# Third tiles of at most 64 tokens at 320 columns with stacked halves, the unit's arms in another order, and rank and table products behind the column transposes

## The chip, the core and the metric

The kernel runs on one core of one Trainium2 chip. A core has a matrix engine (TensorE: PE for the products, PEld for the loads of their stationary operand), VectorE (DVE), ScalarE (ACT), GpSimd (POOL) and SyncE (SP), each with its own list of instructions, which wait for one another by semaphores; a memory on the chip, a separate accumulator memory that the products write, and 16 DMA engines to the large memory. The metric is the device time of one execution in microseconds (us), lower is better. The time before is the median of three executions: 659.64 us (659.41 to 659.84).

## The reference

Eight batches of eight heads, 512 tokens and 32 state rows of 64 numbers go through attention in both directions. The 4,352 rows that come out (512 wide) go through a mixture of eight experts, each row to the one expert that wins.

```python
scores = scale * np.matmul(x, state.transpose(0, 1, 3, 2))      # softmax over the 32 state rows
xread = np.matmul(a, state)
scores2 = scale * np.matmul(state, x.transpose(0, 1, 3, 2))     # softmax over the 512 tokens
sread = np.matmul(a2, x)
...
e_idx = np.argmax(logits, axis=1)                                # logits = x @ w_gate, 8 experts
gate_w = probs[np.arange(N), e_idx]                              # probs = softmax of logits
eom = 1.0 / (1.0 + np.exp(-(x @ w_output_gate)))
for e in range(E):
    mask = e_idx == e
    h = np.maximum(x[mask] @ w1[e], 0.0)                         # 512 -> 1024
    ye = h @ w2[e]                                               # 1024 -> 512
    out[mask] = gate_w[mask, None] * eom[mask, e, None] * ye
```

With the inputs of this case the experts get 1568, 632, 512, 541, 513, 40, 0 and 546 rows.

## The kernel before

**Attention.** A loop over eight batches. In PE's list an iteration has, by line: transposes of x (L325) and of the softmax over the columns (`e2_trans`, L419), scores (L337), transposes of the row softmax (`a_trans`, L359), transposes of the scores for the column softmax (`columns_softmax`, L401), reads by the states (`state_reads`, L431), reads by the tokens (`token_reads`, L380 to L382) and the state rows' output (L444). The results go to a table `xa` in the large memory, one row per token, with the row's gate factor behind it.

**Routing** runs along with it. `route` takes the logits of a batch, finds each row's expert, and counts by matmul how many rows ahead of it have the same expert (the rank product: L243, L245 and L247, a triangle of ones and ones against the one-hot rows). From rank and expert two one-hot matrices are made, and a product of 128 x 272 (the table product, L300) adds every row's number into the table `tid_ps` of lists by expert. `route` is a generator: `go_on` lets it run a piece further at certain points of the iteration. A scheduler sets the order of this part of the program on each engine by its own estimates, so a rank product may stand between the scores.

**Experts.** An expert's rows are cut in tiles of 128; tiles are grouped into units of two, the last unit of an expert with an odd number of tiles takes three, and an expert with one tile makes a unit of one. Here 17 units run, with 2, 2, 2, 2, 2, 3 | 2, 3 | 2, 2 | 2, 3 | 2, 3 | 1 | 2, 3 tiles. The number of tiles of a unit (`size`) is read from the memory into registers of the engines, so what a unit does is chosen by branches on the chip, and the program holds every arm of every unit. The order of this part is the one it is written in (`manual_schedule`).

`unit` (L697 to L727) has, in order: `first`, the first product of all tiles of the unit at once (eight blocks of 12 matmuls, each half of the number format against each: 384 columns for three tiles, 256 otherwise), with a ReLU on ACT that writes the rounded upper half `hhi` and a subtraction on DVE that writes the lower half `hlo` for each block; the fetches of the next expert's weights (SP) and the gather of the rows for the unit after the next (POOL); `second` for tile 0, with the transposes of the next unit's rows in it; transposes; `second` for tile 1 and tile 2, each under a branch. `second` (L668 to L682) is 24 matmuls of 512 columns for one tile of 128 rows, then ACT scales the result by the row's factor and POOL scatters 128 rows to the output. Where an arm is not taken, `nothing` (L660) does one tiny product and copy, so that all arms use the same buffers. Up to 13 units are certain; four more that may not run lie behind branches (`rest`, L729 to L733).

The arms of the first product before, in PE's list: the arm for three tiles first, then the jump over the other.

```python
with tc.If(size == 3) as odd:
    first(u, NTOKU, chg)
with odd.Else():
    first(u, 2 * P, chg)
```

Of the kernel before, what the change touches and what calls it, by code (L numbers as in the profile page):

```python
# [21 lines left out]
def attention_then_top1_experts(ctx: ExitStack, tc: tile.TileContext, x, state, w_gate, w_og, w1, w2, out):  # L22
# [60 lines left out]
    unit_f = const.tile([1, NU], F32, name="unit_f")  # L83
    nc.gpsimd.tensor_copy(unit_f, un_i)

    def after(inst, before):
# [32 lines left out]
    with ExitStack() as actx:  # L119
# [101 lines left out]
        def route(lgs, nch, tile0, write):  # L221
# [20 lines left out]
            rkv = rk[:, : nch * E].rearrange("p (c e) -> p c e", e=E)  # L242
            nc.tensor.matmul(rkv, lhsT=tri, rhs=ohb, start=True, stop=False)  # L243
            for c in range(nch - 1):
# [44 lines left out]
            for c0 in range(0, nch, 3):  # L289
                ops = []  # L290
                for c in range(c0, min(nch, c0 + 3)):
                    last = len(done) >= NT - 5
                    pa = asm.tile([P, P], F32R, name="pa", tag="pal" if last else "pa", bufs=5 if last else 3)
                    (nc.gpsimd if last else nc.vector).tensor_scalar(pa, iota_q[:, :P], rf[:, 0, c : c + 1], None, op0=ALU.is_equal)
                    rb = asm.tile([P, NQ], F32R, name="rb", tag="rbl" if last else "rb", bufs=5 if last else 3)
                    nc.vector.tensor_scalar(rb, iota_q, col[:, c, :], vid[:, tile0 + c : tile0 + c + 1], op0=ALU.is_equal, op1=ALU.mult)
                    ops.append((pa, rb))
                yield
                for pa, rb in ops:
                    done.append(nc.tensor.matmul(tid_ps, lhsT=pa, rhs=rb, start=(len(done) == 0), stop=(len(done) == NT - 1)))  # L300

        st = {}
# [92 lines left out]
        def columns_softmax(b):  # L395
# [3 lines left out]
            for g in range(NG):  # L399
                for c in range(NC):  # L400
                    nc.tensor.transpose(tp[:, g, P * c : P * c + P], s_v[:, c, g, :], ident)  # L401
            st2 = asm.tile([P, 3, NG], F32, name="st2", tag="st2")
# [21 lines left out]
        def state_reads(b):  # L424

            xb, e2T = xbs[b], st["e2T", b]
            sr = pss.tile([P, 512], F32, name="pss", tag="pss")
            srv = sr.rearrange("p (h k n) -> p h k n", h=H, k=2)
            for h in range(H):
                for cc in range(2):  # L430
                    nc.tensor.matmul(srv[:, h], lhsT=xb[:, h, 2 * cc : 2 * cc + 2, :].rearrange("p c d -> p (c d)"),  # L431
                                     rhs=e2T[:, 2 * cc : 2 * cc + 2, NS * h : NS * h + NS], start=(cc == 0), stop=(cc == 1))
            t2, bb = b // 4, b % 4
            for k in range(2):
                nc.vector.tensor_copy(srT[D * k : D * k + D, :, NS * bb : NS * bb + NS], srv[D * k : D * k + D, :, k, :])
# [95 lines left out]
        r1 = slice(0, 1)  # L531
        nc.vector.scalar_tensor_tensor(ODD[r1], in0=LONE[r1], scalar=-2.0, in1=ODD[r1], op0=ALU.mult, op1=ALU.add)
        nc.vector.tensor_scalar(LAST[r1], SUM[r1], 1.0, None, op0=ALU.subtract)
        uni = unit_f.rearrange("o (s k) -> o s k", k=1).broadcast_to([1, NU, E])
# [61 lines left out]
    hhi = bp1.tile([P, KH, NTOKU], F32R, name="hhi")  # L596
    hlo = bp1.tile([P, KH, NTOKU], F32R, name="hlo")
    rest_of = bp1.tile([P, 8], F32, name="rest_of")
    stage_tile(bp1, 1)
# [41 lines left out]
    def first(u, n, chg):  # L641

        hi, lo = xT_all[u % 2]
        for fb in range(KH):
# [7 lines left out]
            if fb in (0, 3):  # L652
                upper(2 if fb == 0 else 3, chg)
            nc.scalar.activation(hhi[:, fb, :n], p1[:, :n], AF.Relu)  # L654
            nc.vector.scalar_tensor_tensor(hlo[:, fb, :n], in0=p1[:, :n], scalar=0.0, in1=hhi[:, fb, :n].bitcast(F32),  # L655
                                           op0=ALU.max, op1=ALU.subtract)
            if fb in (1, 4):
# [8 lines left out]
    def second(u, t, between=None):  # L666
        po = py.tile([P, DM], F32, name="po", tag="po")
        c = slice(P * t, P * t + P)  # L668
        for j in (2, 3):
# [6 lines left out]
            for k in range(4):  # L676
# [5 lines left out]
                                     in_=y, in_offset=None)  # L682

    def values(u):
        if u >= NU:
            return None
        size = nc.values_load(route_i[0:1, 0, u : u + 1], engines=[ET.PE, ET.Activation, ET.DVE, ET.Pool], min_val=0, max_val=3,
                              skip_runtime_bounds_check_because="2, with one more for an odd number's last tile, or one less for an only one")
        if u == 0:
# [7 lines left out]
    def unit(u):  # L697
        size, chg, nxt = val[u]
        with tc.If(size == 3) as odd:
            first(u, NTOKU, chg)  # L700
        with odd.Else():
            first(u, 2 * P, chg)
        val[u + 1] = more = values(u + 1)
        for i in (2, 3):
# [9 lines left out]
        if more:  # L714
            x_transposed(u + 1, 1)
            with tc.If(more[0] == 3) as three:  # L716
                x_transposed(u + 1, 2)
            with three.Else():
                nothing(ph, "p1")
        with tc.If(size >= 2) as two:  # L720
            second(u, 1)
        with two.Else():
            nothing(py, "po")
        with tc.If(size == 3) as three:  # L724
            second(u, 2)
        with three.Else():
            nothing(py, "po")  # L727

    def rest(u):  # L729
# [44 lines left out]
```

## Time and profile before

| | |
|---|---|
| time, median of three executions | 659.64 us (659.41 to 659.84) |
| profiled execution | 661.41 us |
| its span | 659.7 us |
| mean granted clock of TensorE | 0.968 |
| PE busy | 615.5 us (93%), 3941 products |
| DVE busy | 283.4 us (43%) |
| ACT busy | 245.3 us (37%) |
| POOL busy | 176.9 us (27%) |
| moved by DMA | 78.57 MB in 46289 packets, mean 119 GB/s |

The profile is one execution, recorded by the hardware. A row of a group or of the timeline names the line of the program, the engine, the operation with what it writes and reads, and then the time for which the engine was idle before it and what ended that. "PE 615.5 (93%)" is the time with at least one product in the array; products are pipelined, so the distance of the starts of two of them is the price of one. PEclk is the clock that the chip granted to TensorE as a share of full speed (0.50 is half). PEq and PEldq are the sequencers of PE: branches, loads of registers and waits stand there. The queues q1 and q0 carry the program's own transfers, q8 and q14 the code.

### The profile page before, as it was taken

What the parts mean: (1) busy time and instruction counts of PE and PEld (TensorE: products, weight loads), DVE (VectorE), ACT (ScalarE), POOL (GpSimd) and SP (SyncE); (2) the same over time, 40 slices, a digit from 0 to 9 for tenths busy, and PEclk for the clock granted to TensorE, in tenths of its full rate; (3) what the DMA queues carried; (4) which work ended last, traced back from release to release, by engine and by line L of the source; (5) the groups of instructions that cost most, each with busy time, mean ns of one, the idle gap of its engine ahead of it and who ended that gap; (6) DMA issues with size and microseconds to landing.
All of it is one profiled execution on the core that took longest, in us unless ns stands there. A gap on an engine that the chain in (4) does not pass through costs nothing. (4 is left out here: it accounts for less than half of the span.)

```text
span 659.7 us, 11415 instructions
## 1 busy us (share of the span) xinstructions
PE 615.5 (93%) x3941; PEld 552.3 (84%) x3941; DVE 283.4 (43%) x622; ACT 245.3 (37%) x411; POOL 176.9 (27%) x254
## 2 busy tenths in 40 slices
PE   7899898998689999999999999999999999999990
PEld 5898797897468998998989989899898998988980
DVE  5547858979863211221235243144132514463210
ACT  3566536556042222222334244244233324472210
POOL 8135505531042221121122203123112220322210
PEclk8999979999779999999999999999999999999996
DMA  8534432322265220220145225326315523475210
GB/s 224 212 128 131 141 119 80 129 69 98 53 229 194 68 82 19 67 83 33 51 161 194 82 83 173 125 80 233 117 52 173 182 82 105 154 249 188 67 35 19
DMA packets 46289, 78.57 MB, mean 119 GB/s; under 512 B 11056, under 2 KB 19248, under 8 KB 46192
## 3 DMA queue, kind: packets, MB, share of 16 engines
q1 hardware_dynamic: 38592, 52.00, 23.9%
q0 software_dynamic: 7600, 25.38, 11.4%
q8 instruction: 49, 0.80, 0.5%
q14 instruction: 48, 0.39, 0.2%
HBM read 101.98 MB, written 19.42 MB: 184 GB/s over the span
## 5 line engine op out<-in xcount | busy, mean ns | idle before, releaser
L655 DVE SCALAR_TENSOR_TENSOR hlo<-p,hhi 128x256 fp32r<-128x256 f32 (+1 forms) x136 | 62.0, 462 | 224.8 <-ACT hhi L654 212.0
L648 PE MATMUL p<-xhi,whi 128*128 128x256 f32 (+1 forms) x544 | 151.0, 300 | 0.9 <-ACT rest_of L664 0.5
L649 PE MATMUL p<-xhi,wlo 128*128 128x256 f32 (+1 forms) x544 | 149.8, 298 | 0.0
L681 POOL DMA_INDIRECT out_dram<-y,idx x38 | 39.4, 1038 | 316.0 <-ACT y L680 228.0
L674 PE MATMUL po<-whi,hhi 128*128 128x512 f32 x304 | 122.6, 403 | 0.0
L675 PE MATMUL po<-wlo,hhi 128*128 128x512 f32 x304 | 120.1, 395 | 0.0
L654 ACT ACTIVATE hhi<-p 128x256 fp32r<-128x256 f32 (+1 forms) x136 | 56.2, 415 | 135.7 <-PE p L651 132.8
L648 PEld LDWEIGHTS p<-xhi,whi 128*128 128x128 f32 x544 | 103.4, 190 | 2.1 <-ACT rest_of L664 1.2
L649 PEld LDWEIGHTS p<-xhi,wlo 128*128 128x128 f32 x544 | 103.3, 190 | 0.3 <-issue 0.2
L651 PE MATMUL p<-xlo,whi 128*128 128x256 f32 (+1 forms) x544 | 95.8, 298 | 0.0
L678 PE MATMUL po<-whi,hlo 128*128 128x512 f32 x304 | 83.2, 395 | 0.0
L607 POOL DMA_INDIRECT xg<-xa,idx x57 | 68.4, 1200 | 49.5 <-issue 16.2
L651 PEld LDWEIGHTS p<-xlo,whi 128*128 128x128 f32 x544 | 81.1, 190 | 0.0
L680 ACT ACTIVATE y<-po,xg 128x512 f32<-128x512 f32 x38 | 26.1, 688 | 132.5 <-issue 49.1
L678 PEld LDWEIGHTS po<-whi,hlo 128*128 128x128 f32 x304 | 57.0, 187 | 14.0
L675 PEld LDWEIGHTS po<-wlo,hhi 128*128 128x128 f32 x304 | 57.2, 188 | 11.6
L674 PEld LDWEIGHTS po<-whi,hhi 128*128 128x128 f32 x304 | 57.1, 188 | 11.5
L635 DVE TENSOR_TENSOR wlo<-stage,whi 128x2048 fp32r<-128x2048 f32 x24 | 54.4, 2286 | 11.6 <-ACT whi L628 11.6
L621 DVE TENSOR_TENSOR xlo<-pxT,xhi 128x512 fp32r<-128x512 f32 x39 | 25.9, 687 | 62.4 <-ACT xhi L620 62.4
L628 ACT CAST whi<-stage 128x2048 fp32r<-128x2048 f32 x24 | 45.1, 1902 | 3.9 <-DVE hlo L655 1.7
L620 ACT CAST xhi<-pxT 128x512 fp32r<-128x512 f32 x39 | 22.2, 583 | 30.7 <-PE pxT L618 30.7
L337 PE MATMUL psb<-sT,xT 128*128 128x64 f32 x256 | 32.7, 289 | 0.2 <-ACT xT L327 0.2
(189 smaller groups left out, 728.2 us busy)
## 6 DMA issues: line engine op xcount, KB each, us to landing
stage<-in_moe_w_dram SPq DMA_DIRECT2D x74, 1024.0 KB
xb<-in_x_dram SPq DMA_DIRECT2D x7, 1024.0 KB
xa<-xm SPq DMA_DIRECT2D x7, 1024.0 KB
xb<-in_x_dram SPq DMA_DIRECT2D x2, 512.0 KB
xa<-xm SPq DMA_DIRECT2D x4, 256.0 KB
xg<-xa,idx POOLq DMA_INDIRECT x57, 3.6
out_dram<-y,idx POOLq DMA_INDIRECT x38, 3.1
sraw<-in_state_dram SPq DMA_DIRECT2D x2, 256.0 KB
```

The source lines that it names most:

```text
L607: g = nc.gpsimd.indirect_dma_start(out=xg_all[u % 3][i], out_offset=None, in_=xa[:, :], in_offset=bass.IndirectOffsetOnAxis(ap=ix, axis=0))
L628: nc.scalar.copy(whi[i], stage[i])
L635: nc.vector.tensor_sub(wlo[i], stage[i], whi[i].bitcast(F32))
L648: nc.tensor.matmul(p1[:, :n], lhsT=whi[i][:, k, c], rhs=hi[:, k, :n], start=(k == 0), stop=False)
L649: nc.tensor.matmul(p1[:, :n], lhsT=wlo[i][:, k, c], rhs=hi[:, k, :n], start=False, stop=False)
L651: nc.tensor.matmul(p1[:, :n], lhsT=whi[i][:, k, c], rhs=lo[:, k, :n], start=False, stop=(k == KX - 1))
L654: nc.scalar.activation(hhi[:, fb, :n], p1[:, :n], AF.Relu)
L655: nc.vector.scalar_tensor_tensor(hlo[:, fb, :n], in0=p1[:, :n], scalar=0.0, in1=hhi[:, fb, :n].bitcast(F32), op0=ALU.max, op1=ALU.subtract)
L674: nc.tensor.matmul(po, lhsT=hhi[:, f, c], rhs=whi[j][:, k, :], start=(f == 0), stop=False)
L675: nc.tensor.matmul(po, lhsT=hhi[:, f, c], rhs=wlo[j][:, k, :], start=False, stop=False)
L678: nc.tensor.matmul(po, lhsT=hlo[:, f, c], rhs=whi[j][:, k, :], start=False, stop=(f == KH - 1))
L681: nc.gpsimd.indirect_dma_start(out=out[:, :], out_offset=bass.IndirectOffsetOnAxis(ap=idx[:, W * u + t : W * u + t + 1], axis=0), in_=y, i ...
```

## The change

Five things change.

1. The routing tail makes a fourth size: 4, where an odd number's last tile has at most 64 rows. Five small DVE operations compute it.
2. A unit of size 4 runs the first product with 320 columns (`FEW`) instead of 384. The ReLU and the subtraction of its last 64 columns write the two halves next to each other into one tile, `hfew` (64 columns upper, 64 lower half).
3. For such a tile `second_few` takes the place of `second`: with the two halves stacked as one stationary operand of 128, 16 matmuls do what 24 did (the product of the two lower halves comes with them). Rows 64 to 127 of the result are copied out by ACT, added to rows 0 to 63 by DVE, scaled by ACT, and 64 rows are scattered.
4. The arms of a unit stand in another order: first the arm for sizes 1 and 2, and in its else-arm the branch between 384 and 320 columns. The same order holds for the small arms (transposes of the next unit's third tile, the third tile's second product).
5. The rank products of all but the last five tiles, and the first 24 table products, are held behind the last column transpose, or the last read by the states, that was written before them. It is an order in PE's list alone, with no wait of its own (`NoSync`).

```diff
+    def behind(inst, before):
+        tc.add_manual_dep(inst.ins, before.ins.name, mybir.DependencyInfo(mybir.DependencyClass.NoSync, mybir.DependencyReason.DATA), reason="order")
...
-            nc.tensor.matmul(rkv, lhsT=tri, rhs=ohb, start=True, stop=False)
+            m = nc.tensor.matmul(rkv, lhsT=tri, rhs=ohb, start=True, stop=False)
+            if len(done) < NT - 5:
+                behind(m, st["pe"])
...
                     done.append(nc.tensor.matmul(tid_ps, lhsT=pa, rhs=rb, start=(len(done) == 0), stop=(len(done) == NT - 1)))
+                    if len(done) < NT - 9:
+                        behind(done[-1], st["pe"])
...
-                    nc.tensor.transpose(tp[:, g, P * c : P * c + P], s_v[:, c, g, :], ident)
+                    st["pe"] = nc.tensor.transpose(tp[:, g, P * c : P * c + P], s_v[:, c, g, :], ident)
...
+            st["pe"] = m
...
+        few = asm.tile([1, 2, E], F32, name="few", tag="few", bufs=1)
+        nc.vector.scalar_tensor_tensor(few[:, 0, :], in0=TILES[r1], scalar=-float(P), in1=cps[r1, :E], op0=ALU.mult, op1=ALU.add)
+        nc.vector.tensor_scalar(few[:, 0, :], few[:, 0, :], -float(P // 2), None, op0=ALU.is_le)
+        nc.vector.tensor_scalar(few[:, 1, :], ODD[r1], 0.0, None, op0=ALU.is_gt)
+        nc.vector.tensor_tensor(few[:, 0, :], few[:, 0, :], few[:, 1, :], op=ALU.mult)
+        nc.vector.tensor_add(ODD[r1], ODD[r1], few[:, 0, :])
...
+    hfew = bp1.tile([P, KH, P], F32R, name="hfew")
+    HP = P // 2
+    FEW = 2 * P + HP
...
-            nc.scalar.activation(hhi[:, fb, :n], p1[:, :n], AF.Relu)
-            nc.vector.scalar_tensor_tensor(hlo[:, fb, :n], in0=p1[:, :n], scalar=0.0, in1=hhi[:, fb, :n].bitcast(F32),
-                                           op0=ALU.max, op1=ALU.subtract)
+            parts = [(hhi[:, fb], hlo[:, fb], 0, n)]
+            if n == FEW:
+                parts = [(hhi[:, fb], hlo[:, fb], 0, 2 * P), (hfew[:, fb, :HP], hfew[:, fb, HP:], 2 * P, FEW)]
+            for th, _, c0, c1 in parts:
+                nc.scalar.activation(th[:, : c1 - c0], p1[:, c0:c1], AF.Relu)
+            for th, tl, c0, c1 in parts:
+                nc.vector.scalar_tensor_tensor(tl[:, : c1 - c0], in0=p1[:, c0:c1], scalar=0.0, in1=th[:, : c1 - c0].bitcast(F32),
+                                               op0=ALU.max, op1=ALU.subtract)
...
+    def second_few(u):
+        po = py.tile([P, DM], F32, name="po", tag="po")
+        for f in range(KH):
+            nc.tensor.matmul(po, lhsT=hfew[:, f, :], rhs=whi[2 + f // 4][:, f % 4, :], start=(f == 0), stop=False)
+            nc.tensor.matmul(po, lhsT=hfew[:, f, :], rhs=wlo[2 + f // 4][:, f % 4, :], start=False, stop=(f == KH - 1))
+        y2 = bp.tile([HP, DM], F32, name="y2", tag="y2", bufs=1)
+        nc.scalar.copy(y2, po[HP:])
+        y = bp.tile([P, DM], F32, name="y", tag="y", bufs=3)
+        nc.vector.tensor_add(y2, y2, po[:HP])
+        nc.scalar.activation(y[:HP], y2, AF.Copy, scale=xg_all[u % 3][2][:HP, DM : DM + 1])
+        nc.gpsimd.indirect_dma_start(out=out[:, :], out_offset=bass.IndirectOffsetOnAxis(ap=idx[:HP, W * u + 2 : W * u + 3], axis=0),
+                                     in_=y[:HP], in_offset=None)
...
-        with tc.If(size == 3) as odd:
-            first(u, NTOKU, chg)
-        with odd.Else():
+        with tc.If(size <= 2) as even:
             first(u, 2 * P, chg)
+        with even.Else():
+            with tc.If(size == 3) as odd:
+                first(u, NTOKU, chg)
+            with odd.Else():
+                first(u, FEW, chg)
...
-        with tc.If(size == 3) as three:
-            second(u, 2)
-        with three.Else():
+        with tc.If(size <= 2) as even:
             nothing(py, "po")
+        with even.Else():
+            with tc.If(size == 3) as odd:
+                second(u, 2)
+            with odd.Else():
+                second_few(u)
```

Lines of the changed program lie some 4 to 40 higher than before: the rank product is at L247 instead of L243, the branch of a unit at L737 and L740 instead of L699, the first product at L667 to L670 instead of L648 to L651.

PE's list in the second iteration of attention, around the rank product (`ohb` is the one-hot of the rows). Before:

```order
L419 MATMUL psb<-ident,e_783 128x128 x8
L337 MATMUL psb<-sT,xT 128x2x32 x4
L243 LDWEIGHTS tri
L243 MATMUL pss<-ohb_859,tri 128x64
...
L247 LDWEIGHTS ones
L247 MATMUL pss<-run_bf,ones 128x64
L337 MATMUL psb<-sT,xT 128x2x32 x12
L359 MATMUL psb<-ident,a_sb 128x128 x8
L431 MATMUL pss<-e2T,xb 128x64 x2
L401 MATMUL psb<-ident,s_sb 128x128 x8
```

The change:

```order
L427 MATMUL psb<-ident,e_783 128x128 x8
L345 MATMUL psb<-sT,xT 128x2x32 x16
L367 MATMUL psb<-ident,a_sb 128x128 x8
L409 MATMUL psb<-ident,s_sb 128x128 x8
L247 LDWEIGHTS tri
L247 MATMUL pss<-ohb_859,tri 128x64
...
L253 LDWEIGHTS ones
L253 MATMUL pss<-run_bf,ones 128x64
L388 MATMUL psb<-sbd_181,aThi 128x272
```

The rank product leaves the middle of the scores and stands behind the column transposes; the reads by the states (L431, now L439) go behind the token reads.

PE's list at the start of the first unit, around the branch on its size. Before:

```order
L699 COMPARE_AND_BRANCH
L648 MATMUL p_2235<-xhi_2175,whi_101 128x384
...
L651 MATMUL p_2344<-xlo_2176,whi_103 128x384 x4
L699 UNCONDITIONAL_BRANCH
L648 MATMUL p_2359<-xhi_2175,whi_101 128x256
```

The change:

```order
L737 COMPARE_AND_BRANCH
L667 MATMUL p_2242<-xhi_2181,whi_101 128x256
...
L670 MATMUL p_2351<-xlo_2182,whi_103 128x256 x4
L737 UNCONDITIONAL_BRANCH
L740 COMPARE_AND_BRANCH
L667 MATMUL p_2367<-xhi_2181,whi_101 128x384
...
L670 MATMUL p_2476<-xlo_2182,whi_103 128x384 x4
L740 UNCONDITIONAL_BRANCH
L667 MATMUL p_2491<-xhi_2181,whi_101 128x320
```

A unit of two tiles took the branch at the start and passed over one arm; now it runs into its arm and its jump at the end passes over two. A unit of three tiles runs through one arm more of branches before it begins.

More of the change, by code (lines that the diff above doesn't have):

```diff
@@ L430, in state_reads @@
                 for cc in range(2):
-                    nc.tensor.matmul(srv[:, h], lhsT=xb[:, h, 2 * cc : 2 * cc + 2, :].rearrange("p c d -> p (c d)"),
+                    m = nc.tensor.matmul(srv[:, h], lhsT=xb[:, h, 2 * cc : 2 * cc + 2, :].rearrange("p c d -> p (c d)"),
                                      rhs=e2T[:, 2 * cc : 2 * cc + 2, NS * h : NS * h + NS], start=(cc == 0), stop=(cc == 1))
+            st["pe"] = m
             t2, bb = b // 4, b % 4
@@ L686, in values @@
             return None
-        size = nc.values_load(route_i[0:1, 0, u : u + 1], engines=[ET.PE, ET.Activation, ET.DVE, ET.Pool], min_val=0, max_val=3,
-                              skip_runtime_bounds_check_because="2, with one more for an odd number's last tile, or one less for an only one")
+        size = nc.values_load(route_i[0:1, 0, u : u + 1], engines=[ET.PE, ET.Activation, ET.DVE, ET.Pool], min_val=0, max_val=4,
+                              skip_runtime_bounds_check_because="2, with one or two more for an odd number's last tile, or one less for an only one")
         if u == 0:
@@ L715, in unit @@
             x_transposed(u + 1, 1)
-            with tc.If(more[0] == 3) as three:
+            with tc.If(more[0] <= 2) as two:
+                nothing(ph, "p1")
+            with two.Else():
                 x_transposed(u + 1, 2)
-            with three.Else():
-                nothing(ph, "p1")
         with tc.If(size >= 2) as two:
@@ L723, in unit @@
             nothing(py, "po")
-        with tc.If(size == 3) as three:
-            second(u, 2)
-        with three.Else():
+        with tc.If(size <= 2) as even:
             nothing(py, "po")
+        with even.Else():
[3 more added lines that the diff above has]
+                second_few(u)
     def rest(u):
```

## The prediction

> **What bounds the kernel now.** I read the page first: busy times, slices and queues.
>
> ```profile
> PE 615.5 (93%) x3941; PEld 552.3 (84%) x3941; DVE 283.4 (43%) x622; ACT 245.3 (37%) x411; POOL 176.9 (27%) x254
> PE   7899898998689999999999999999999999999990
> PEclk8999979999779999999999999999999999999996
> q8 instruction: 49, 0.80, 0.5%
> ```
>
> PE carries the span. The slices show two regions: attention with its routing (slices 1 to 12), where PE has gaps and the clock drops, and the expert units, where every slice is at 9. The stretches of the units, asked for by window (length, then busy time and instructions of PE, PEld, DVE, ACT, POOL, clock, DMA share, GB/s), say it sharper:
>
> ```profile
> 200.00:300.00 100.00, 100.00 (x654) 89.52 (x653) 21.70 (x44) 23.97 (x59) 21.83 (x21) 1.00 0.24 81
> 309.44:326.17 16.73, 16.73 (x98) 16.73 (x98) 3.90 (x7) 4.28 (x9) 3.88 (x4) 1.00 0.21 65
> 343.94:355.24 11.30, 11.30 (x97) 11.30 (x96) 7.11 (x9) 6.76 (x10) 4.80 (x4) 1.00 0.57 183
> 338.34:343.94 5.60, 5.60 (x26) 4.50 (x25) 0.00 (x0) 0.69 (x1) 0.98 (x1) 1.00 0.49 190
> ```
>
> PE has no idle moment there, so whatever PE no longer does in a unit shortens the span one for one, and whatever stops PE lengthens it one for one. The second row is a first product of 384 columns, the third one of 256, the fourth the second product of a third tile.
>
> **The columns.** A first product is 96 matmuls: 16.73/96 = 0.174 us each at 384 columns, 11.30/96 = 0.118 at 256. At 320 I take the middle, 0.146: 2.71 us less per unit. A second product of a third tile is 24 matmuls in 5.60, 0.233 each; the stacked form has 16, so 1.87 less. Five units run a third tile; four of them have a last tile of at most 64 tokens (32, 29, 1 and 34; the fifth has 120). Gain: 4 × 2.71 = 10.9 and 4 × 1.87 = 7.5, together **-18.4**. For 320 columns no row exists; the price lies between the two neighbours, but the spacing follows the columns so closely (0.174/0.118 = 1.47 for 1.5) that I leave it at ±1.
>
> **The extra halves.** In those units each block has a second ReLU on ACT and a second subtraction on DVE.
>
> ```profile
> L655 DVE SCALAR_TENSOR_TENSOR hlo<-p,hhi 128x256 fp32r<-128x256 f32 (+1 forms) x136 | 62.0, 462 | 224.8 <-ACT hhi L654 212.0 <-ACTq L627 12.6
> L621 DVE TENSOR_TENSOR xlo<-pxT,xhi 128x512 fp32r<-128x512 f32 x39 | 25.9, 687 | 62.4 <-ACT xhi L620 62.4
> 644.17 0.69 ACT L680 ACTIVATE y<-po,xg 128x512 f32<-128x512 f32 x1 [4.90 <-PEq L731]
> ```
>
> A block lasts 12 × 0.146 = 1.75 us on PE; twice 0.46 on DVE fits below it with half its time left, so I cost it at nothing. Its cover is PE's own block and the four buffers of the first product; without that it would be 8 × 0.46 = 3.7 us per unit. The new copy and add behind the stacked product are hidden too, except in the last unit, where they stand between the last matmul and the last scatter: a copy at ACT's 0.69 and an add at DVE's 0.69, **+1.4**. The five small DVE operations of the routing tail work on eight numbers while PE waits for gathers: nothing.
>
> **Attention.** PE's timeline (start, duration, what it waited for) and the windows around it:
>
> ```profile
> 77.45 1.09 PE L419 MATMUL psb<-ident,e 128*128 128x128 f32 x8 [1.21 <-ACT xm L383]
> 81.11 0.19 PE L243 MATMUL pss<-ohb,tri 128*128 128x64 bf16 x1 [1.64 <-DVE ohb L235]
> 74.47:77.88 3.41, 2.20 (x21) 1.96 (x20) 1.88 (x5) 2.32 (x4) 3.41 (x6) 1.00 0.21 72
> 77.88:81.30 3.42, 1.78 (x23) 1.60 (x21) 3.21 (x10) 2.25 (x3) 3.12 (x7) 1.00 0.79 270
> 81.30:91.54 10.24, 10.24 (x57) 10.24 (x54) 6.41 (x24) 2.30 (x3) 1.23 (x6) 0.50 0.40 123
> 26.68:30.10 3.42, 3.40 (x31) 3.16 (x30) 2.82 (x7) 2.20 (x3) 1.58 (x9) 1.00 0.02 5
> 30.10:33.51 3.41, 1.71 (x16) 1.71 (x17) 2.50 (x2) 1.64 (x3) 1.65 (x1) 1.00 0.00 0
> PE psb L382 <- DVE aTlo L363: 3.2, 4, 1.2
> ```
>
> In the second iteration the rank product (L243) stands in the middle of the scores and holds the twelve scores behind it for 1.64 us. Two stretches with a mean busy share of (2.20+1.78)/6.83 = 0.58 follow each other, and then the clock stands at 0.50 for 10.24 us, which is 5.1 lost; at 26.68 the pair's mean is (3.40+1.71)/6.83 = 0.75 and the clock stays. With the rank product behind the column transposes the wait goes, and the pair's mean rises to (3.98+1.64)/6.83 = 0.82, above both. Gain 1.64 + 5.1 = 6.7. What is late next: the token reads come sooner and meet their operand (0.8 us a wait, the last row), so **-6.0**. The ends: -6.7, or, if the other wait (1.21) grows and the clock drops all the same, -1.6; and +1.7 if a rank product that now comes later makes as long a wait further on.
>
> **The order of the arms.** Before, a two-tile unit takes the branch at its start and passes over one arm; now it runs through and passes over two at its end. That is the term that decides.
>
> ```profile
> L731 PEldq COMPARE_BRANCH  x6: 68/72/4042, 528.3 to 644.4; - x6
> L699 PEldq COMPARE_BRANCH  x22: 63/290/432, 188.3 to 623.1; - x22
> 626.19 0.39 PE L674 MATMUL po<-whi,hhi 128*128 128x512 f32 x1
> L724 PEldq COMPARE_BRANCH  x1: 217/217/217, 445.5 to 445.5; - x1
> q1 hardware_dynamic: 363, 0.71, 89.2%
> q8 instruction: 1, 0.02, 5.5%
> 450.15 0.19 PEld L649 LDWEIGHTS p<-xhi,wlo 128*128 128x128 f32 x1 [0.15 <-issue]
> q1 hardware_dynamic: 759, 1.52, 103.8%
> ```
>
> Code reaches the sequencer in packets of 0.80 MB/49 = 16 KB. PE's program up to the end of the last unit that runs has some 12,240 instructions (products and weight loads counted apart), so a packet holds about 256. All branches of the units cost 63 to 432 ns (L699) but one: the branch that ends the last unit and passes over four units that do not run, about nine packets away, took **4042 ns** (L731). Branches of less than a packet find their target loaded: the packet behind the current one is fetched while this one runs. I laid a grid of 256 instructions over PE's program; with one offset all the branches that step over a line of it are followed by their packet. The row at 450.15 shows the same from the other side: at 445.5 a branch (L724) entered a new packet, none was delivered until 447.7 (the row of q1 is 445.5 to 447.7, that of q8 447.7 to 448.8: the transfers of weights filled the engines), and PE paused at 450.15, just where the next packet begins.
>
> An arm is 96 products and 96 weight loads, so two arms with their branches are about 390 instructions, 1.53 packets. On the same grid, carried to the changed program, eight of the twelve jumps behind a first product of 256 columns or less land two packets on (units 0, 1, 2, 6, 8, 12, 14 and 15 of 0 to 16), and unit 9's lands in a packet whose fetch has just begun: nine stalls. Before there is none of them inside a unit.
>
> The cover: the sequencer runs ahead of the array. The last branch of L699 starts at 623.1 and the first matmul behind it at 626.19: 3.1 us, or 18 matmuls of 0.174. Of 256 columns that is 18 × 0.118 = 2.1 us. One stall then shows 4.04 - 2.1 = 1.9 us: 9 × 1.9 = **+17.1**.
>
> That price is from a stretch with little traffic. These are the windows from each of the nine jumps on, in the run before (units 0, 1, 2, 6, 8, 9, 12, 14, 15; the last two numbers are DMA share and GB/s):
>
> ```profile
> 200.40:203.40 3.00, 3.00 (x24) 2.84 (x23) 2.05 (x4) 0.77 (x2) 1.91 (x1) 1.00 0.94 344
> 224.00:227.00 3.00, 3.00 (x24) 2.85 (x23) 1.02 (x3) 0.77 (x2) 0.00 (x0) 1.00 0.00 0
> 247.60:250.60 3.00, 3.00 (x24) 2.83 (x23) 1.02 (x3) 0.77 (x2) 0.00 (x0) 1.00 0.04 8
> 353.10:356.10 3.00, 3.00 (x24) 2.86 (x23) 2.05 (x4) 0.77 (x2) 0.00 (x0) 1.00 0.88 322
> 411.50:414.50 3.00, 3.00 (x24) 2.83 (x23) 2.05 (x4) 0.77 (x2) 0.00 (x0) 1.00 0.85 320
> 435.10:438.10 3.00, 3.00 (x23) 2.83 (x23) 1.02 (x3) 0.77 (x2) 0.00 (x0) 1.00 0.04 14
> 517.20:520.20 3.00, 3.00 (x24) 2.86 (x23) 2.06 (x4) 0.77 (x2) 0.00 (x0) 1.00 0.89 341
> 575.60:578.60 3.00, 3.00 (x23) 2.82 (x23) 2.05 (x4) 0.77 (x2) 0.00 (x0) 1.00 0.99 373
> 594.80:597.80 3.00, 3.00 (x24) 2.87 (x23) 2.04 (x4) 0.77 (x2) 2.00 (x1) 1.00 0.99 360
> ```
>
> Six of the nine (shares 0.85 to 0.99) fall into the weight transfers of a new expert, as the packet of 445.5 did. A code packet waits there: 2.2 us at 445.5, and 3.8 us behind the first unit's branch at 188.3 (no packet on q8 from 188.3 to 192.1, the row of q1 with 759), where a whole fetch, its return included, takes 4.04 otherwise. I take 1.2 us more for each of the six, **+7.2** (ends: nothing; 2.8 each, +16.8). In the four units with 320 columns two branches follow each other over an arm each, 1.52 packets together; most of that is inside PE's lead, I take half a microsecond each, **+2.0** (0 to 4). As lower end of the nine a fetch whose return is shorter than the 4042 ns holds: 1.3 us each, 11.7.
>
> [...]
>
> **Sum.** -18.4 - 6.0 + 1.4 + 17.1 + 7.2 + 2.0 = **+3.3 us**. The profiled execution took 661.41, its span 659.7; so 664.7 there, and on the median of 659.64, **663 us**. A difference of 0.2%, 1.3 us, is what a measurement of this kernel can tell from none.
>
> **The rivals.**
>
> Deeper code memory: packets two ahead are there, no stall. -18.4 - 6.0 + 1.4 = -23.0: 636.6. For it: only one branch of before is long, and it goes nine packets. Against it: the pause at 450.15, where the very next packet was not there, and the packets that follow a branch one by one. 0.10.
>
> Faster although it stalls: a jump's price decides, and the balance point is 23.0/9 = 2.55 us shown per jump, 4.65 with the cover. If the code packet is served between the weights' packets (the pause at 450.15 was only short), each of the nine shows 1.3 to 1.9 and nothing is added: -23.0 + 11.7 to 17.1 = -11.3 to -5.9, some 651. Against it: the waits of 2.2 and 3.8 us. 0.27.
>
> The stalls take the clock along: a gap of 4.04 + 1.2 - 2.1 = 3.1 us inside two windows leaves (6.83 - 3.1)/6.83 = 0.55, below the 0.58 behind which the clock halved at 81.30. A window at half clock costs 1.7 us, three cost 5.1. Six gaps with one window each: +10.2, 673; with three each 694. For it that pair of rows; against it that a gap of 1.9 leaves 0.72, near the pair that did not drop, and that one pair makes no threshold. 0.20.
>
> The attention keeps its clock drop (the first wait of 1.21 grows): only -1.6 there, 663 + 4.4 = 667. 0.08.
>
> My own sum holds 0.35, with a range of 655 to 670: the loaded surcharge from 0 to 2.8 for six, and part of a clock loss.
>
> **How the numbers follow.** Faster by over 0.2% is the first two rivals nearly whole (0.36) and the low end of my own case (0.05): 0.41. Within 0.2%: 0.10, from my own case's lower half. Slower: 0.49. The range leaves out the deeper memory (0.10), the low edge of the balance case and the longest clock losses: 645 to 678.
>
> **What would show it.** First products of 320 columns last 14.0 us and the stacked second 3.7 (wrong: more than half a microsecond off, or five units still with 384). A branch of L737 at about 4 us behind units 1, 2 and 9 and 5 us behind 0, 6, 8, 12, 14 and 15, and PE gaps of 1.9 and 3.1 before the first L698 of these units; 636 and no such branch would end my reasoning. The share of PE in the slices of the units below 9, and PEclk below 9 there for the clock rival. In attention no wait of the rank product (L247) at 81 and a clock of 1.00 in 81 to 91. The last scatter 1.4 us further behind the last matmul.

## The result and the profile after

The changed kernel takes **686.56 us** (median, 683.50 to 688.22), against 659.69 for the kernel before in the same comparison: ratio 1.0399, 95% interval 1.0367 to 1.0431, 4% slower. Forecast were 663 us and a range of 645 to 678. The sign was right, the size far off: +26.9 us where +3.3 was forecast. The profiled execution took 684.99 us with a span of 683.2, 23.5 more than the span before. The working below adds up to these 23.5.

The page after: busy times, slices of the span, and code transfers.

```profile
PE 608.6 (89%) x3909; PEld 543.7 (80%) x3909; DVE 286.5 (42%) x663; ACT 248.0 (36%) x447; POOL 177.8 (26%) x254
PE   7899988998689999999997998999999799797990
PEclk8999989999689999999999999999999999998996
q8 instruction: 65, 1.06, 0.7%
```

PE is busy for 6.9 us less than before and the span is 23.5 us longer: the time went into gaps, and the slices show them as 7s among the 9s in the units. The waits of PE in the units say where (line waited at, releaser, total, times, longest):

```profile
PE po L698 <- issue: 24.3, 6, 4.7
PE po L698 <- ACTq L646: 2.9, 2, 1.5
PE po L698 <- ACT hhi L677: 1.3, 1, 1.3
```

Nine waits, all at L698, the first matmul of `second`, which stands behind the arms: 28.5 us. Before, the units had 0.9 us of waits altogether. "issue" says that no data was waited for. The two other names are what the view takes for the releaser when something else happened to end just then. The sequencer's branches at three of the nine places, units 1, 6 and 14, and the array's gap at unit 6:

```profile
L737 PEldq COMPARE_BRANCH  x1: 3257/3257/3257, 228.5 to 228.5; - x1
L737 PEldq COMPARE_BRANCH  x1: 6266/6266/6266, 357.1 to 357.1; - x1
L737 PEldq COMPARE_BRANCH  x1: 6571/6571/6571, 588.5 to 588.5; - x1
363.85 0.77 PE L698 MATMUL po<-whi,hhi 128*128 128x512 f32 x1 [4.50 <-issue]
```

The trace has three more long branches (3.1 to 3.5 us, L740, at 314.5, 485.1 and 545.6) at the start of units of 320 columns, and two shorter ones (1.8 and 2.8 us, L737, at 279.1 and 632.9). Behind each of the five PE waits at most 0.5 us.

By unit, from the starts of the first and second products in both timelines, the 23.5 us fall into these parts:

| part | forecast | measured |
|---|---|---|
| first products, four units of 320 columns | -10.9 | -10.0 |
| second products of the same units | -7.5 | -7.4 |
| first unit begins (attention and routing) | -6.0 | -0.8 (188.76 to 187.97) |
| stalls of units 1, 2 and 9 (quiet) | +5.7 | +4.7 |
| stalls of units 0, 6, 8, 12, 14 and 15 (under weights) | +18.6 | +25.0 |
| half clock behind the stalls | 0 | +9.9 |
| other branches and small waits in the units | +2.0 | +1.2 |
| behind the last matmul | +1.4 | +0.9 |
| sum | +3.3 | +23.5 |

### The profile page after: what moved, and what is told of

Same layout as the page of the kernel before. It is cut to its first block, busy times and chain, and to the rows that moved or that the text cites. A ratio compares the mean times of both kernels' runs of the same rounds, so it can differ in the third digit from the quotient of the medians.

```text
span 683.2 us, 11668 instructions
## 1 busy us (share of the span) xinstructions
PE 608.6 (89%) x3909; PEld 543.7 (80%) x3909; DVE 286.5 (42%) x663; ACT 248.0 (36%) x447; POOL 177.8 (26%) x254
## 3 DMA queue, kind: packets, MB, share of 16 engines
q8 instruction: 65, 1.06, 0.7%
## 5 line engine op out<-in xcount | busy, mean ns | idle before, releaser
L667 PE MATMUL p<-xhi,whi 128*128 128x256 f32 (+2 forms) x544 | 145.9, 293 | 2.1 <-PE po L687 1.0
L668 PE MATMUL p<-xhi,wlo 128*128 128x256 f32 (+2 forms) x544 | 144.8, 291 | 0.0
L698 PE MATMUL po<-whi,hhi 128*128 128x512 f32 x272 | 114.9, 422 | 28.6 <-issue 24.3
L679 DVE SCALAR_TENSOR_TENSOR hlo<-p,hhi 128x256 fp32r<-128x256 f32 (+1 forms) x136 | 57.0, 430 | 186.5 <-ACT hhi L677 118.8
L705 POOL DMA_INDIRECT out_dram<-y,idx x34 | 34.7, 1020 | 323.2 <-ACT y L704 238.2
L699 PE MATMUL po<-wlo,hhi 128*128 128x512 f32 x272 | 111.2, 409 | 0.0
L667 PEld LDWEIGHTS p<-xhi,whi 128*128 128x128 f32 x544 | 103.3, 190 | 3.6 <-issue 1.7
L670 PE MATMUL p<-xlo,whi 128*128 128x256 f32 (+2 forms) x544 | 92.1, 291 | 0.0
L698 PEld LDWEIGHTS po<-whi,hhi 128*128 128x128 f32 x272 | 53.2, 196 | 41.0 <-issue 25.4
L670 PEld LDWEIGHTS p<-xlo,whi 128*128 128x128 f32 x544 | 78.4, 189 | 0.0
L702 PE MATMUL po<-whi,hlo 128*128 128x512 f32 x272 | 76.0, 402 | 0.0
L702 PEld LDWEIGHTS po<-whi,hlo 128*128 128x128 f32 x272 | 52.3, 192 | 13.0
L699 PEld LDWEIGHTS po<-wlo,hhi 128*128 128x128 f32 x272 | 53.6, 197 | 10.8
L439 PE MATMUL pss<-e2T,xb 128*128 128x64 f32 x256 | 30.1, 274 | 0.4 <-DVE t L265 0.4
```

Of the source, the lines that this page charges most:

```text
L667: nc.tensor.matmul(p1[:, :n], lhsT=whi[i][:, k, c], rhs=hi[:, k, :n], start=(k == 0), stop=False)
L668: nc.tensor.matmul(p1[:, :n], lhsT=wlo[i][:, k, c], rhs=hi[:, k, :n], start=False, stop=False)
L670: nc.tensor.matmul(p1[:, :n], lhsT=whi[i][:, k, c], rhs=lo[:, k, :n], start=False, stop=(k == KX - 1))
L679: nc.vector.scalar_tensor_tensor(tl[:, : c1 - c0], in0=p1[:, c0:c1], scalar=0.0, in1=th[:, : c1 - c0].bitcast(F32), op0=ALU.max, op1=ALU.s ...
L698: nc.tensor.matmul(po, lhsT=hhi[:, f, c], rhs=whi[j][:, k, :], start=(f == 0), stop=False)
L699: nc.tensor.matmul(po, lhsT=hhi[:, f, c], rhs=wlo[j][:, k, :], start=False, stop=False)
```

## The experiments

My theory now: a jump over 1.5 code packets stops PE's sequencer; the price is a fetch, longer while weights are under way, less PE's lead; gaps take the clock along. Rivals: it is the new order as such, whatever the length of the jump; it is the 320 columns and the stacked form; it is the hold in attention.

**The order of two arms alone.** The kernel before with its two arms swapped.

```diff
-        with tc.If(size == 3) as odd:
-            first(u, NTOKU, chg)
-        with odd.Else():
-            first(u, 2 * P, chg)
+        with tc.If(size <= 2) as even:
+            first(u, 2 * P, chg)
+        with even.Else():
+            first(u, NTOKU, chg)
```

> The kernel before with the two arms of the first product in the changed order alone: 256 columns first, 384 in the else-arm. A two-tile unit jumps at the end of the 256 columns here too, but over one arm, 0.76 packets. Theory (only a jump past the next packet stalls): 659 to 662 us, no gap over 0.5 us, no branch over 0.5 us inside the units. Rival (a jump at the end of the 256 columns costs whatever its length, since PE's lead is only 2.1 us there): 675 us and more, gaps behind all twelve.

659.72 us, ratio 1.0005 (0.9993 to 1.0016). The branches of the units:

```profile
L699 PEldq COMPARE_BRANCH  x29: 67/179/420, 185.0 to 601.9; - x29
```

None is over 0.42 us. The order as such costs nothing here, and neither does a jump of 0.76 packets at the end of 256 columns.

**The third arm and the order, without the gain.** The flag of size 4 is multiplied by zero.

```diff
+        nc.vector.tensor_scalar(few[:, 0, :], few[:, 0, :], 0.0, None, op0=ALU.mult)
         nc.vector.tensor_add(ODD[r1], ODD[r1], few[:, 0, :])
```

> The changed kernel with size 4 never chosen (its flag is multiplied by zero): code and arms are those of the change, the third tiles take 384 columns and 24 products as before. Theory (320 columns and stacked halves save 17.4 us, all of the loss is in the jumps): 686.6 + 17 to 18 = 700 to 706 us, the same nine gaps. Rival (the stacked form itself costs): below 690.

694.2 us, ratio 1.0523 (1.0500 to 1.0546): 7.6 us above the changed kernel, where 17 to 18 were expected. The rival falls, since the kernel is slower without the stacked form. But the gain is less than half of what the columns are worth, and that was a miss. The timelines say why. The branch of unit 6 and the start of the megabyte of weights that is under way then, first in the changed kernel, then in this one:

```profile
L737 PEldq COMPARE_BRANCH  x1: 6266/6266/6266, 357.1 to 357.1; - x1
L658 SPq DMA_DIRECT2D stage<-in_moe_w_dram x1: 378/378/378, 355.6 to 355.6; - x1
```

```profile
L738 PEldq COMPARE_BRANCH  x1: 4669/4669/4669, 360.1 to 360.1; - x1
L659 SPq DMA_DIRECT2D stage<-in_moe_w_dram x1: 377/377/377, 357.2 to 357.2; - x1
```

And the queues (packets, megabytes, share of the 16 engines). From the issue of the megabyte up to the code packet, 355.6 to 360.8 of the changed kernel and 357.2 to 362.2 of this one, the code queue has no packet, and the weights' queue moves:

```profile
q1 hardware_dynamic: 532, 1.06, 59.5%
```

```profile
q1 hardware_dynamic: 500, 1.02, 65.9%
```

The code packets that these jumps wait for, from 360.8 to 362.0 of the changed kernel, and from 362.2 to 363.4 of this one:

```profile
q1 hardware_dynamic: 184, 0.38, 90.2%
q8 instruction: 1, 0.02, 5.7%
```

```profile
q1 hardware_dynamic: 53, 0.08, 63.7%
q8 instruction: 1, 0.02, 5.8%
```

The packet starts at 360.8 in the changed kernel and at 362.3 here: 5.2 and 5.1 us after the megabyte was issued, when 1.06 and 1.02 MB have moved. So in these two traces it waits until that megabyte is all but through. Behind a unit of 320 columns the jump comes 1.5 us after the issue, behind one of 384 it comes 2.9 us after it, and the branch is 1.6 us shorter. Units 12 and 14, the other ones behind a short third tile, go the same way (gaps of 4.35 and 4.74 in the changed kernel, 3.07 and 2.79 here). The saved columns bring the next jump nearer to the start of the weights, and the stall takes part of the saving back: 4.9 us at these three units, of the 9.1 that are missing between the two profiled executions. Of the rest, 1.5 us is an earlier start of the first unit in this execution, 0.9 the shorter end without the copy and the add, and 1.8 lies in half clock and small waits.

**The same jump at another place.** The arms turned round, so that a two-tile unit steps over both other arms at its start.

```diff
-        with tc.If(size <= 2) as even:
-            first(u, 2 * P, chg)
-        with even.Else():
+        with tc.If(size >= 3) as large:
             with tc.If(size == 3) as odd:
                 first(u, NTOKU, chg)
             with odd.Else():
                 first(u, FEW, chg)
+        with large.Else():
+            first(u, 2 * P, chg)
```

> The changed kernel with the arms of the first product turned round: sizes 3 and 4 first, the 256 columns in the else-arm. The program is as long and a two-tile unit steps over the same 1.5 packets of code, but at its start, behind products of 512 columns, where PE's lead is 18 times 0.233 = 4.2 us, and not at the end of the 256 columns, where it is 2.1. Theory (a code packet is waited for, and PE's lead covers 4.2 of the 3.3 to 6.5 us): gaps of 0 to 2 us, 3 to 6 us in all in place of 28.6, no clock loss in the units, 645 to 653 us. Rival (the length of a jump counts, not where it stands, or 320 columns and stacked halves cost by themselves): 680 to 687.

663.80 us, ratio 1.0055 (1.0030 to 1.0081): much better than the change, outside the 645 to 653 that the theory gave. Its branches, and what PE waited for:

```profile
L737 PEldq COMPARE_BRANCH  x17: 67/3312/6252, 186.4 to 612.6; - x17
PE p L667 <- issue: 12.7, 3, 6.2
PE p L668 <- issue: 3.0, 2, 2.8
```

Half of the seventeen branches take 3.3 us and more. With those of L738, twelve branches in the units take 3 us and more, as many as in the change with its L740. Yet PE shows five waits at the first products, and four of them are long. Between products of 512 columns the lead, an estimated 4.2 us (18 products of 0.233), covers a quiet fetch: the branches of 3.3 us at 215.4 and 239.1 leave no wait. What is left stands where no lead is: 6.2 us ahead of the first unit, 5.2 behind unit 14, which has one tile and ends on two tiny products, and 1.3 and 2.8 inside the first products of units 3 and 10. By the count of instructions these two units land 29 and 12 instructions short of a packet's end, so I take it that they run into the next packet before it is there; no run tests this apart. I had overlooked the first unit and the one-tile unit.

**Shifting the code.** A branch ahead of the first unit that never runs, with 54 tiny products in it.

```diff
+        with tc.If(n_units > NU - 1) as never:
+            ps = ph.tile([P, 512], F32, name="p1", tag="p1")
+            for _ in range(54):
+                nc.tensor.matmul(ps[:, :8], lhsT=ones, rhs=ones[:, :8], start=True, stop=True)
+            nc.scalar.copy(rest_of, ps[:, :8])
+        with never.Else():
+            nothing(ph, "p1")
```

> The changed kernel with a branch that never runs ahead of the first unit: 56 tiny products with their loads, which push all later code of PE by 112 to 113 instructions (0.44 of a packet) and run nothing. Theory (256 instructions a packet, on the grid found in the run before): the stalls move to units 3, 4, 10 and 12, and 9 at the edge; the jumps of units 0, 1, 2, 6, 8, 14 and 15 fall to 0.3 to 0.5 us. Gaps of 12 to 17 us in place of 28.6, 664 to 674 us. Rival (what stalls belongs to the unit and not to the place of its code): the nine gaps of before, 684 to 689.

673.43 us, ratio 1.0199 (1.0180 to 1.0218). (The text above says 56 products; it is 54, and the branches with them make up the 112.) The waits:

```profile
PE po L698 <- issue: 17.8, 5, 4.5
PE po L698 <- ACTq L646: 3.3, 2, 1.7
PE po L702 <- issue: 1.6, 1, 1.6
```

By their times they are at units 0, 3, 4, 6, 9, 10, 12 and one of 1.6 us in 15. Units 1, 2, 8 and 14 have lost their gaps, and 3, 4 and 10 have new ones, without any change in what they compute. So the place of the code decides. The sum was missed (22.7 us of gaps, not 12 to 17), and units 0 and 6, whose gaps were to go, kept them. That the time still fell into 664 to 674 is luck. On the shifted grid units 0 and 6 step over one line only, but their jumps stand 26 and 3 instructions behind a line, so I take it that the packet of the next one had hardly been asked for; no run tests this apart. That is the case that I had counted for unit 9 in the prediction.

**No weights under way.** The transfers of the later experts' weights are never started.

```diff
-            fetch(i, chg == 1 if u else None, nxt if u else next0)
+            fetch(i, chg > 1 if u else None, nxt if u else next0)
...
-                fetch(i, more[1] == 1, more[2])
+                fetch(i, more[1] > 1, more[2])
```

> The changed kernel without the transfers of weights from the second change of expert on: their condition is never true, so the later experts are computed with old weights. Program, arms and sizes stay. Theory (code packets wait behind the weights): unit 0 keeps its gap of 3.7 us, all other gaps fall to 1.3 to 1.6 us, 14 to 17 us in all; without gaps of 3.4 us and more there is at most the clock loss behind unit 0; 660 to 666 us. Rival (the long gaps come from the place in the program): gaps of 4 us and more stay at units 6, 12, 14 and 15, 680 to 687.

668.89 us, ratio 1.0110 (1.0065 to 1.0154).

```profile
PE po L698 <- ACTq L646: 11.1, 6, 2.4
PE po L698 <- issue: 7.5, 3, 3.9
```

Unit 0 keeps 3.9 us. At units 6, 8, 12, 14 and 15 the gaps of 4.5, 3.0, 4.4, 4.7 and 4.0 us have become 1.6, 2.0, 2.4, 2.0 and 2.0. That the weights lengthen the fetch is thereby shown. All gaps together are 18.6 us, not 14 to 17. The time is 3 us above the upper end that was expected: the gaps of four units stayed 0.3 to 0.8 us longer than 1.6, for a reason that I did not look for, and two gaps of 2 us (units 14 and 15) took the clock along: their windows have a busy share of 0.43 and 0.44, and half clock follows. The 3.4 us of the expectation is no bound that a run shows: it lies between the gaps of the changed kernel that left half clock behind them (3.7 us and more) and the longest that did not (3.0), and here the 2 us went below it.

**The arm of 256 columns in the middle.** 384, 256, 320: a two-tile unit steps over one arm at its start and one at its end.

```diff
-        with tc.If(size <= 2) as even:
-            first(u, 2 * P, chg)
-        with even.Else():
-            with tc.If(size == 3) as odd:
-                first(u, NTOKU, chg)
-            with odd.Else():
+        with tc.If(size == 3) as odd:
+            first(u, NTOKU, chg)
+        with odd.Else():
+            with tc.If(size <= 2) as even:
+                first(u, 2 * P, chg)
+            with even.Else():
                 first(u, FEW, chg)
```

> The changed kernel with the arm of 256 columns between the other two: 384, 256, 320. A two-tile unit steps over one arm at its start and over one at its end, 0.76 packets each; only unit 7 (384 columns) jumps over two, behind columns with 3.1 us of lead. Theory: gaps of 2 to 9 us in all, mostly where a packet has just been entered, at most one clock loss in the units; 642 to 652 us, faster than the kernel before. Rival (any second jump in a unit costs what the one of the change costs): 665 and more.

649.35 us, ratio 0.9847 (0.9827 to 0.9868): faster than both kernels, by 10.3 us and by 37. The page and the waits:

```profile
PE 596.9 (92%) x3909; PEld 535.2 (83%) x3909; DVE 285.1 (44%) x663; ACT 247.9 (38%) x447; POOL 169.7 (26%) x254
PE   7899979997689999999999999999999999969990
PE p L668 <- issue: 3.2, 1, 3.2
PE po L698 <- ACT hhi L677: 1.0, 1, 1.0
```

None of the nine gaps is left at its place. There are two others: 1.0 us at unit 7, the one unit that jumps over two arms at its end, and 3.2 us inside the first product of unit 15, which follows the unit of one tile. Branches of 3.3 to 3.6 us are still there (303.0, 416.3 and 518.7), at the start of units behind products of 512 columns; PE waits at most 0.4 us behind them. The computation is the same as in the change, product for product. Only the place of three arms in the program differs.

**The order 320, 256, 384.** It ran on one chip with three kernels below: the order 384, 256, 320 once more, the hold alone in more rounds, and the order 384, 256, 320 without the hold. The edit is shown against the order 384, 256, 320.

```diff
-        with tc.If(size == 3) as odd:
-            first(u, NTOKU, chg)
+        with tc.If(size == 4) as odd:
+            first(u, FEW, chg)
...
-                first(u, FEW, chg)
+                first(u, NTOKU, chg)
```

> The changed kernel with the arms in the order 320, 256, 384: the two-tile units keep one arm to step over at their start and one at their end; the four units of 320 columns now jump over two arms at their end, where PE's lead is 18 times 0.146 = 2.6 us, and the weights are not under way. By the grid one of these four, unit 13, jumps past the next packet (a gap near 1 us). Theory: 647 to 651 us. Rival (four longer jumps cost 1 us or more each): 652 to 655.

650.11 us, ratio 0.9850 (0.9823 to 0.9878): no different from the order 384, 256, 320 on that chip (650.84, the next run). The one jump of a short unit that was expected to stall did, behind the 320 columns of unit 13:

```profile
536.89 0.47 PE L698 MATMUL po<-whi,hhi 128*128 128x512 f32 x1 [0.93 <-ACT hfew L677]
```

**That order once more**, unchanged.

> The changed kernel with the arms in the order 384, 256, 320 once more, for a comparison on one chip with the next two. 648 to 651 us.

650.84 us, ratio 0.9863 (0.9835 to 0.9891).

**The hold in attention.** It was tried in three ways. First, out of the changed kernel:

```diff
-                behind(m, st["pe"])
+                pass
...
-                        behind(done[-1], st["pe"])
+                        pass
```

> The changed kernel without the fifth part: the attention's order is that of before, sizes, arms and stacked halves stay. Theory (the loss comes from the units alone): 685 to 689 us, gaps of 1.3 to 4.7 us in PE at the end of the first product of units 0, 1, 2, 6, 8, 9, 12, 14 and 15. Rival (the hold of the rank product is part of the loss): below 680.

687.23 us, ratio 1.0407 (1.0381 to 1.0433), with gaps of 1.4 to 4.7 us at the same nine units: the loss is in the units.

Second, alone, in the kernel before (the lines of `behind`, its two calls and the two settings of `st["pe"]` from the diff of the change, nothing else):

> The kernel before with only the fifth part of the change: rank and table products held behind the column transposes and the reads by the states. In the changed kernel the first unit began only 0.8 us sooner than before (187.97 against 188.76). Theory (the hold removes one wait and moves the clock loss to later places): 658 to 660 us, the wait at 81 gone, half clock at 94 and again near 159. Rival (the hold is worth the 6 us that was forecast and the changed kernel lost them by chance): 653 to 654.

657.61 us, ratio 0.9977 (0.9949 to 1.0005). Its trace has no half clock at 81, 3.4 us of it at 94.9 and none near 159. In more rounds:

> The kernel before with the hold alone, in more rounds. Theory: 657 to 659 us, ratio 0.996 to 0.999. Rival (no difference): a ratio whose interval holds 1.000 in its middle. The 6 us that were forecast: 0.991.

659.27 us, ratio 0.9988 (0.9969 to 1.0007). Third, the order 384, 256, 320 without the hold (the edit of the first way):

> The same arms without the fifth part of the change (rank and table products are not held). Theory (the hold is worth what the kernel with the hold alone showed, some 1 to 3 us): 650 to 653 us. Rival (the 2.5 us of that kernel were scatter): 648 to 650, like the kernel with the hold.

651.71 us, ratio 0.9879 (0.9850 to 0.9907), 0.9 us above the same kernel with it. All of these differences point to a gain, by the ratios 0.5 to 1.5 us; none is clear of the intervals, so the sign is not settled. The 6 us that were forecast are excluded.

## Why the prediction was wrong

**The columns** (-18.4) held: a first product of 320 columns took 14.15 us (14.45 in the last unit) for the forecast 14.0, and the stacked second form saved 1.86 us per unit for 1.87.

```profile
317.84:331.99 14.15, 14.15 (x96) 14.15 (x97) 3.89 (x14) 4.29 (x16) 3.89 (x4) 1.00 0.27 79
```

The extra operations of DVE and ACT hid as forecast; PE is busy throughout.

**The order of the arms** held as a mechanism, to the unit: the nine jumps that were named are the nine behind which PE stood still, and moving the code moved the gaps. In the changed kernel each of the nine jumps, 1.53 packets long, took 3.2 us and more; jumps of 0.76 packets in the kernel with its two arms swapped took at most 0.42. Packets two ahead, which the first rival took to be there, were not there at these nine places. The quiet price was 1.3 to 1.5 us per gap, not 1.9: the branches took 3.2 to 3.3 us here, less than the 4042 ns of the one row that I had.

**The step that failed first is the term "the loaded surcharge".** I took 1.2 us for each of six, with 2.8 as the upper end, after two packets that were 2.2 and 3.8 us late. That made gaps of 3.1 us. Measured are 4.05, which is 2.6 over a quiet gap: six loaded gaps of 3.7, 4.5, 3.0, 4.4, 4.7 and 4.0 us, 24.3 together, mean 4.05, against the quiet three, mean 1.41; in the unit times the six make 25.0 us. That is near the upper end. What I had not done is ask when the megabyte in the way starts: the packet comes 5.2 to 6.0 us after its issue, so the price follows from the distance of the jump to it, and the change itself shortens that distance behind three of its short units.

**The second, and by size the largest, is the clock, a term that I left at zero in the sum and priced as a rival** ("a window at half clock each: +10.2"). It came: 9.9 us. Even by the condition that I wrote, a gap of 3.1 us left a share of 0.55, below the 0.58 that had halved the clock, and I gave it 0.20 all the same. The condition was wrong, too. I took the mean of two windows; the traces show a single one to decide. In the trace of the changed kernel half clock comes and goes on one grid of 3.41 us: it lasts 3.4 us from 206.5, 363.5, 534.2 and 595.6, 6.8 from 93.9 and 619.5, and 10.2 from 172.4. Three cases on such grids, each a window with the one behind it: the changed kernel at unit 6, its unit 1, and the kernel with shifted code at unit 9.

```profile
360.09:363.50 3.41, 0.00 (x0) 0.00 (x0) 0.18 (x1) 0.00 (x0) 0.64 (x1) 1.00 1.04 386
363.50:366.91 3.41, 3.06 (x7) 2.48 (x8) 0.00 (x0) 0.00 (x0) 0.00 (x0) 0.50 0.53 193
230.38:233.79 3.41, 1.99 (x11) 1.54 (x10) 0.42 (x1) 0.38 (x1) 0.00 (x0) 1.00 0.03 10
233.79:237.20 3.41, 3.41 (x19) 2.78 (x18) 0.69 (x1) 0.59 (x1) 0.00 (x0) 1.00 0.01 2
```

```profile
442.90:446.31 3.41, 1.58 (x9) 1.23 (x9) 0.52 (x2) 2.13 (x2) 0.00 (x0) 0.99 0.04 10
446.31:449.73 3.42, 3.42 (x10) 2.53 (x9) 3.23 (x2) 1.95 (x2) 0.00 (x0) 0.51 0.00 0
```

A window with no busy time, and one with 1.58 of 3.41 us, are followed by one at 0.50; the one with 1.99 is not. The mean of two does not separate the cases: 0.56 and 0.58 were not followed by half clock (the changed kernel, 421.53 to 428.35, and the kernel with shifted code, unit 0, where the single windows had 0.45 and 0.55), and 0.72 and 0.75 were (the kernel without transfers at unit 14, and the second run of 384, 256, 320 at 569.6, single windows 0.43 and 0.51). So 1.8 us of idle time in one window cost as much clock at unit 9 of the shifted code (the next window at 0.51) as the gap of 4.5 at unit 6 of the changed kernel (0.50). Five of the six loaded gaps left such a window behind. The exclusion that I wrote down, that a gap of 1.9 us leaves enough, does not hold.

**Attention** (-6.0) was wrong. The wait at the rank product did go and so did the half clock behind it:

```profile
83.56 0.19 PE L247 MATMUL pss<-ohb,tri 128*128 128x64 bf16 x1
81.30:91.54 10.24, 8.63 (x73) 7.63 (x72) 9.59 (x26) 7.45 (x13) 4.37 (x16) 1.00 0.30 102
```

But both came back further on. The reads by the states now stand behind the token reads, and what follows them waits for their result; the clock halves there:

```profile
94.72 0.69 PE L453 MATMUL psb<-idw,srT 128*128 128x80 f32 x2 [1.83 <-DVE srT L444]
90.43:93.85 3.42, 2.46 (x23) 2.32 (x21) 3.39 (x9) 1.41 (x4) 3.12 (x6) 1.00 0.65 240
93.85:100.67 6.82, 5.95 (x28) 5.98 (x29) 6.51 (x20) 1.18 (x3) 4.96 (x8) 0.50 0.67 193
158.70:162.12 3.42, 3.42 (x17) 3.42 (x16) 2.88 (x20) 1.79 (x4) 0.00 (x0) 0.50 0.29 108
```

6.82 us at half clock stand against 10.24 before, and in this execution another 3.4 us follow near 159, so the sum is the same. I had forecast an upper loss of the same form ("as long a wait further on", +1.7) and given it no weight. The order of the two programs showed the reads by the states (L439) behind the token reads; I had quoted that and not asked who waits for them.

The larger part of the term, 5.1 us of half clock, was also no fixed property of the kernel before. The kernel with its two arms swapped has the same attention and the same wait of 1.64 us at the rank product, but there the edges of the windows cut the idle time in another place (shares of 0.59 and 0.86, against 0.65 and 0.52 before), and the clock stayed at 1.00:

```profile
80.84 0.19 PE L243 MATMUL pss<-ohb,tri 128*128 128x64 bf16 x1 [1.64 <-DVE ohb L235]
76.93:80.35 3.42, 2.02 (x16) 1.84 (x17) 3.01 (x8) 2.94 (x4) 3.16 (x7) 1.00 0.59 218
80.35:83.76 3.41, 2.92 (x33) 2.92 (x33) 3.25 (x21) 0.26 (x1) 1.87 (x7) 1.00 1.01 320
```

So the term took from one execution what another one does not have.

**How it went together.** Of the 20.2 us between the forecast +3.3 and the measured +23.5 the clock is 9.9, the loaded stalls are 6.4 and attention is 5.2; the other terms together are 1.3 the other way. Each miss lay inside the ends that I had written for it: 16.8 for the surcharge, the clock rival's 673, 1.6 or less for attention. I treated them as separate cases with one price each. They are not separate: a longer surcharge makes a longer gap, and a longer gap takes the clock (in the changed kernel the five of 3.7 us and more did, the one of 3.0 and the three quiet ones did not). The range should have been built from the sum of the bad ends (3.3 + 9.6 + 10.2 + 4.4 = 27.5 on the median, 687) and not from the worst single one. That this sum comes so near the measured 686.6 is partly luck: it takes the milder bad end of attention and leaves out the upper end of the four units' branches.

## What to carry to other kernels

In a program with many arms, the place of an arm in the code is a cost: count the instructions that the usual path steps over, and keep every jump shorter than one code packet (0.76 packets took at most 0.42 us with the two arms swapped, 1.53 packets 3.2 us and more in the change), or put it where the sequencer is far ahead (behind 512 columns in the order 384, 256, 320 branches of 3.3 to 3.6 us left waits of at most 0.4). A shorter jump is no guarantee: that order, in which all but unit 7 step over one arm at a time, has these branches still. By the count of instructions other jumps stalled here where they stood just behind the start of a packet (units 0 and 6 of the shifted code, 26 and 3 instructions behind it) or landed just short of the end of one (units 3 and 10 with the arms turned round, 1.3 and 2.8 us). Look at the branches' own durations in the trace, since the waits of the array call these gaps "issue". When several costs have the same cause, add their bad ends before choosing a range.

## What was not expected

- The fetch of code waited behind bulk transfers. In the changed kernel a quiet jump out of the loaded packets took 3.2 to 3.3 us, and 4.8 to 6.6 us with weights under way, and the packet started 5.2 to 6.0 us after the megabyte ahead of it was issued.
- One window of 3.41 us with less than about half its time busy was enough for half clock in the next. In the units of all fourteen traces, windows at full clock with a share below 0.45 were always followed by half clock, and those of 0.52 and more never; from 0.45 to 0.51 five were and four were not (0.45 at unit 8 of the changed kernel was not, 0.51 ahead of unit 15 in the second run of 384, 256, 320 was). In attention, where transposes and narrow products fill the time, a window with a share of 0.72 (90.43 of the changed kernel) was followed by half clock too and one with 0.50 (30.10 of the kernel before) was not, so there the busy share does not tell.
- The lead of the sequencer hid a stall almost wholly behind 512 columns: with the arms turned round, branches of 3.3 us in quiet stretches (215.4 and 239.1) showed nothing in the array.
